# Half of the last product of a gated layer in seven quarter products instead of eight

## The chip, the cores and the metric

The kernel is written in Bass with Tile for one core of a Trainium2 chip: one launch, one core. The metric is the device time of a run in microseconds (us). Three runs of the kernel before were timed.

## What is computed

Three layers follow each other: a causal linear attention with decay, a soft mixture of experts, and a gated two-layer network. The change lies in the last one, whose input `x` (3072 tokens by 512) is the mixture's output `c @ slot_out` with 32 slots, so that the first product of the network has an inner rank of 32.

```
def _moe2_ref(x, w_in, w_out) -> np.ndarray:      # x 3072x512, w_in 512x2048, w_out 2048x512
    h = x @ w_in
    g = h * (1.0 / (1.0 + np.exp(-1.702 * h)))
    return (g @ w_out).astype(np.float32)
```

Both weights arrive as 64-bit floats.

## The kernel before

The first half of the program (attention and experts, up to about 162 us) is the same in both kernels. The rest is the last layer.

- **Splitting.** TensorE multiplies in fp32r, a rounded fp32. To keep precision, each factor is split into a rounded part (hi) and the remainder (lo), and three of the four products are formed: hi·hi, hi·lo, lo·hi.
- **Units.** The 3072 tokens are 6 blocks `b` of 512 (`NB`), the 2048 inner columns 16 tiles `f` of 128 (`KFF`). A unit `(b, f)` is one `h_unit` and one `o_unit`. `h_unit` forms h for 128 inner columns and 512 tokens with one matmul of 512 columns (`gst`, which holds `slot_out @ w_in` in hi and lo, against the softmax weights `cT`); ScalarE applies the gate twice, into `gh` (rounded) and `gg` (fp32). `lo_unit` has VectorE form `gl = gg - gh`. `o_unit` adds, for each of four tiles of 128 tokens, three matmuls of 512 columns to the sums `acc` in PSUM. That is 13 matmuls for each of 96 units.
- **Order.** `units` takes for each block first the tiles below `FA[b]` (2 for block 0, 4 for the others), whose sums are kept in `part`, then for each block the remaining tiles; `add_out` adds `part` to them and stores. h of unit u is issued two units ahead of its `o_unit`.
- **Narrowing.** `narrow` turns a piece of 64-bit weights into fp32 by three bit operations on VectorE (L151, L153, L155). For `w_out`, ScalarE then rounds it (L556) and GpSimd forms the remainder (L559). `work(budget)`, called between `h_unit` and `lo_unit` of each unit, takes such steps from a queue with costs until the budget `BUD` is used up. The raw weights come by DMA through three buffers. `make_g1` and `make_g2` make four tiles of `gst` at a time from narrowed `w_in`.
- **PSUM** has 8 banks: five in turn for `acc`, three for h and for small things.

Of the kernel before, what the change touches and what calls it, by code (L numbers as in the profile page):

```python
# [19 lines left out]
DM = H * D  # L20
# [16 lines left out]
FA = (2, 4, 4, 4, 4, 4)  # L37
# [5 lines left out]
BUD = 1.9  # L43
CW = (0.4, 0.6, 0.6, 0, 0.6)
# [4 lines left out]
def retention_soft_moe_mlp(  # L49
# [513 lines left out]

    def win_ops(j, z, k0=0, k1=KDM, f0=0, f1=256):
# [4 lines left out]

    units = [(b, f) for b in range(NB) for f in range(FA[b])] + [(b, f) for b in range(NB) for f in range(FA[b], KFF)]  # L570

    def h_unit(u):
        b, f = units[u]
        hp = pf.tile([P, 512], F32, tag="h", name=f"h{u}", bufs=3)
        mm(hp, lhsT=gst[:, f * P:(f + 1) * P], rhs=cT[:, 512 * b:512 * b + 512], start=True, stop=True)  # L575
        gh = fp.tile([P, 512], F32R, tag="gh2", name=f"gh{u}")
        nc.scalar.activation(out=gh, in_=hp, func=AF.Gelu_apprx_sigmoid)  # L577
        gg = fp.tile([P, 512], F32, tag="gg", name=f"gg{u}")
        nc.scalar.activation(out=gg, in_=hp, func=AF.Gelu_apprx_sigmoid)  # L579
        gl = fp.tile([P, 512], F32R, tag="gl2", name=f"gl{u}")  # L580
# [6 lines left out]
    def add_out(b, t, c, a, store=True):  # L587
        ob = part[b][:, t, c]
        nc.vector.tensor_tensor(out=ob, in0=a[:, c], in1=ob, op=ALU.add)  # L589
        if store:  # L590
            r0 = b * 512 + t * P
            nc.sync.dma_start(out=out[r0:r0 + P, c], in_=ob)

    def o_unit(u, t0=0, t1=4, terms=(0, 1, 2)):
        b, f = units[u]
        _, gh, gl = g_hl[u]
        whi, wlo = wh[f], wl[f]
        first, last = f in (0, FA[b]), f in (FA[b] - 1, KFF - 1)
# [13 lines left out]
        split = u == len(units) - 1  # L612
        if split:
            add_out(b, 3, slice(0, DM), acc[3], store=False)
        for t in range(t0, t1 - 1 if split else t1):
# [3 lines left out]
            if f == FA[b] - 1:  # L619
# [343 lines left out]
```

## Time and profile before

| | |
|---|---|
| three runs | 462.16, 463.09, 465.32 us; median 463.09 |
| profiled execution, span from first to last instruction | 462.1 us |
| last layer, from its first h matmul | 162.2 us to the end |
| TensorE busy | 448.5 us, 97% of the span |
| VectorE, ScalarE, GpSimd busy | 220.2, 169.9, 69.6 us |

The page gives no time of its own for the profiled execution beside the span; the fastest run shown is 0.06 us above that span, the median 1.0 us. A busy TensorE is not a TensorE at its peak, since matmuls are pipelined: the pace is read from the starts of neighbouring matmuls.

### The profile page before, as it was taken

To read this page: it belongs to the slowest core of one execution; us is meant where nothing else is said; L and a number is where in the kernel's file an instruction comes from. 1 tells how busy PE (TensorE), PEld (TensorE's weight loads), DVE (VectorE), ACT (ScalarE), POOL (GpSimd) and SP (SyncE) were. 2 spreads that over 40 slices of the span, in tenths; PEclk is the share of its full clock that TensorE was granted. 3 is DMA by queue.
4 is the path that set the end of the run, shared out by engine and by line. 5 is a ranking of instruction groups with operands and counts; after the bars stand their busy time and mean duration, and the time that the engine had idled before them with its cause. 6 is when DMAs were issued, how large, how long until landed. Compare 5 with 4: busy or idle time off the path is not lost.

```text
span 462.1 us, 8629 instructions
## 1 busy us (share of the span) xinstructions
PE 448.5 (97%) x3572; PEld 347.9 (75%) x3572; DVE 220.2 (48%) x412; ACT 169.9 (37%) x342; POOL 69.6 (15%) x69
## 2 busy tenths in 40 slices
PE   8899999999999989999999999999999999999996
PEld 5687877877334468788888888888888888888885
DVE  2355665755465479869396424224224224224223
ACT  2233232333121265665663533333333333333330
POOL 3253443533000112210222200000000000000000
PEclk9899999999999999999999999999999999999999
DMA  8999999999899654725231002002002002002002
GB/s 297 406 354 408 369 396 406 356 404 349 321 423 400 271 193 172 262 84 196 96 116 67 0 1 92 1 0 92 1 0 92 0 0 92 0 2 91 0 1 91
DMA packets 23527, 79.73 MB, mean 173 GB/s; under 512 B 2560, under 2 KB 4000, under 8 KB 19904
## 3 DMA queue, kind: packets, MB, share of 16 engines
q1 hardware_dynamic: 23088, 78.65, 45.3%
q8 instruction: 28, 0.46, 0.4%
q10 hardware_dynamic: 288, 0.36, 0.3%
q0 software_dynamic: 112, 0.16, 0.1%
q14 instruction: 11, 0.09, 0.1%
HBM read 72.88 MB, written 6.29 MB: 171 GB/s over the span
## 4 chain that ended last, share of the span: by engine, by line
PE 85%; DMA 10%; DVE 1%; SPq 1%; issue 1%; ACT 1%; POOL 1%; DVEq 0%; ACTq 0%; POOLq 0%
PE acc L606 56%; DMA qt<-qt_dram 8%; PE h L575 5%; PE sc L199 4%; PE eo L499 3%; PE hp L474 3%; PE y L248 3%; PE y L244 2%; PE xp L269 2%; DMA ktv_first<-ktv_dram 1%; PE st L256 1%; PE op L355 1%; PE tq L510 1%; PE lp L301 1%; PE gp L531 1%
## 5 line engine op out<-in xcount | busy, mean ns | idle before, releaser
L606 PE MATMUL acc<-wo_hl,gh 128*128 128x512 f32 x766 | 236.9, 391 | 0.7 <-ACT gh L577 0.7
L606 PEld LDWEIGHTS acc<-wo_hl,gh 128*128 128x128 f32 x766 | 142.8, 188 | 30.9 <-ACT gh L577 1.0
L606 PE MATMUL acc<-wo_hl,gl 128*128 128x512 f32 x383 | 148.8, 390 | 0.3 <-DVE gl L585 0.3
L585 DVE TENSOR_TENSOR gl<-gg,gh 128x512 fp32r<-128x512 f32 x96 | 66.6, 693 | 151.0 <-ACT gg L579 150.9
L577 ACT ACTIVATE gh<-h 128x512 fp32r<-128x512 f32 x96 | 57.5, 599 | 153.7 <-PE h L575 151.9
L606 PEld LDWEIGHTS acc<-wo_hl,gl 128*128 128x128 f32 x383 | 71.9, 188 | 15.8 <-DVE gl L585 0.7
L579 ACT ACTIVATE gg<-h 128x512 f32<-128x512 f32 x96 | 57.0, 594 | 0.0
L203 DVE TENSOR_TENSOR pt<-sc,ca_t 128x512 f32<-128x512 f32 x44 | 28.3, 686 | 22.3 <-PE sc L199 22.3
L575 PE MATMUL h<-cT,gst 128*128 128x512 f32 x96 | 37.4, 392 | 0.2 <-DVE gst L525 0.2
L559 POOL TENSOR_TENSOR wo_hl<-wf,wo_hl 128x512 fp32r<-128x512 f32 x16 | 21.2, 1345 | 100.5 <-ACT wo_hl L556 100.5
L199 PEld LDWEIGHTS sc<-qt,ktv 64*128 64x128 f32 x320 | 20.2, 192 | 10.8 <-issue 7.0
L199 PE MATMUL sc<-qt,ktv 64*128 64x128 f32 x320 | 23.9, 290 | 4.3 <-DMA qt<-qt_dram 3.8
L225 POOL TENSOR_TENSOR tb<-ca_t 128x512 f32<-128x512 f32 x19 | 19.9, 1048 | 45.4 <-DVE xT L260 45.4
L248 PE MATMUL y<-pt,vt 128*64 128x128 f32 x352 | 24.1, 279 | 0.0
L217 POOL TENSOR_TENSOR vt<-ktv,ca_t 128x512 f32<-128x512 f32 x20 | 20.8, 1042 | 13.3 <-DMA ktv<-ktv_dram 5.0
L258 ACT COPY s_sb<-st 128x256 f32<-128x256 f32 x20 | 7.4, 372 | 39.6 <-PE st L256 39.6
L248 PEld LDWEIGHTS y<-pt,vt 128*64 128x64 f32 x352 | 18.8, 136 | 3.8 <-issue 3.2
L575 PEld LDWEIGHTS h<-cT,gst 128*128 128x128 f32 x96 | 18.0, 188 | 4.7 <-DVE gst L525 1.0
L280 ACT COPY x<-xp 128x512 f32<-128x512 f32 x23 | 13.5, 587 | 11.6 <-PE xp L269 5.0
L260 DVE TENSOR_TENSOR xT<-y,tb 128x512 f32<-128x512 f32 x19 | 13.1, 691 | 9.3 <-PE y L248 9.1
L589 DVE TENSOR_TENSOR part<-acc,part 128x512 f32<-128x512 f32 x24 | 15.1, 684 | 3.6 <-PE acc L606 3.6
L269 PE MATMUL xp<-cb_t,xT 128*128 128x128 f32 x96 | 15.7, 286 | 0.0
(160 smaller groups left out, 366.7 us busy)
## 6 DMA issues: line engine op xcount, KB each, us to landing
w<-w_dram SPq DMA_DIRECT2D x36, 512.0 KB, 7.6
w<-w_dram SPq DMA_DIRECT2D x14, 1024.0 KB, 8.6
ktv<-ktv_dram SPq DMA_DIRECT2D x20, 512.0 KB, 8.4
wi<-w_in_dram SPq DMA_DIRECT2D x7, 1024.0 KB, 5.0
wo<-w_out_dram SPq DMA_DIRECT2D x7, 1024.0 KB, 4.8
out_dram<-part SPq DMA_DIRECT2D x23, 256.0 KB, 2.2
qt<-qt_dram SPq DMA_DIRECT2D x21, 256.0 KB, 6.4
kt<-kt_dram SPq DMA_DIRECT2D x12, 256.0 KB, 7.6
```

The source lines that it names most:

```text
L199: mm(sc[hh][:, a, :], lhsT=kT[hh * D:(hh + 1) * D, a, :], rhs=q_[hh * D:(hh + 1) * D, a, :], start=True, stop=True)
L203: nc.vector.tensor_tensor(out=pt[hh], in0=sc[hh], in1=mask[:, None, :].to_broadcast([P, NP, P]), op=ALU.mult)
L217: nc.gpsimd.tensor_tensor(out=vt, in0=v_, in1=vs[:, c, :, None].to_broadcast([P, H, D]), op=ALU.mult)
L225: nc.gpsimd.tensor_tensor(out=tb_t[i], in0=tab, in1=gsc[:, :, c, None].to_broadcast([P, NP, P]), op=ALU.mult)
L248: mm(out_(a, hh ^ (a & 1)), lhsT=vt[:, 2 * a + (hh ^ (a & 1)), :], rhs=pt[hh ^ (a & 1)][:, a, :], start=(c == 0 and a < 2), stop=True, ski ...
L269: nc.tensor.transpose(xp[:, a * P:(a + 1) * P], xT_t[i][:, a, :], ident)
L559: nc.gpsimd.tensor_tensor(out=l, in0=w, in1=h.bitcast(F32), op=ALU.subtract)
L575: mm(hp, lhsT=gst[:, f * P:(f + 1) * P], rhs=cT[:, 512 * b:512 * b + 512], start=True, stop=True)
L577: nc.scalar.activation(out=gh, in_=hp, func=AF.Gelu_apprx_sigmoid)
L579: nc.scalar.activation(out=gg, in_=hp, func=AF.Gelu_apprx_sigmoid)
L585: nc.vector.tensor_tensor(out=gl, in0=gg, in1=gh.bitcast(F32), op=ALU.subtract)
L606: mm(acc[t], lhsT=g[:, t * P:(t + 1) * P], rhs=w, start=first and n == 0, stop=n == 2 and (last or (u == len(units) - 2 and t == 3)))
```

## The change

The inner tiles 0 to 7 keep their plain units. For the tiles 8 to 15 (`SF0` on) the product `g @ w_out` is formed in Winograd's variant of Strassen's scheme: a square of two inner tiles by 256 tokens by 512 output columns is cut into 2x2 quarters, and seven products of sums of quarters take the place of eight.

- A new unit `("s", (e, j))` covers a block `e` of 256 tokens (12 of them) and a pair `j` of inner tiles (`NSP` = 4): 48 units. `s_h` makes two h matmuls of 256 columns, ScalarE applies the gate once into four quarters of `F_`, VectorE forms four sums of them; `s_round` (ScalarE) rounds seven quarters, `s_lo` forms their remainders: for the first four such units on VectorE alone, then two of seven on GpSimd and five on VectorE. `s_prod` issues 7 products of 3 matmuls with 256 columns each.
- The seven sums of a block stay in PSUM over the four pairs, in half banks (`HALF`): even blocks in banks 0 to 3, odd ones in 3 to 6; h has bank 7. `s_copy` and `s_combine` join them on ScalarE and VectorE into `X_` while the next block runs, and a GpSimd DMA with `accum_op` adds `X_` to the output in HBM, for ten of twelve blocks.
- The weights of the pairs need sums too: `w_sums` on GpSimd (four of 256 columns), then `w_hi` on ScalarE and `w_lo` on GpSimd for seven quarters.
- The order is now: 42 plain units (`runs`: the sums of each run go through `sg` to HBM by a DMA from ScalarE's queue, or by an accumulating one from GpSimd's), then the 48 new units, then the 6 plain units left of block 0, which end the program with `part`, `X_` and the accumulators.
- Narrowing is done in pieces of 1024 columns instead of two of 512; `BUD` falls from 1.9 to 1.2, and the steps that follow a piece on ScalarE and GpSimd are dealt out to later units (`at`, `due`). Each load is issued when a buffer is used up instead of all at once.

The diff, cut to its core:

```
-FA = (2, 4, 4, 4, 4, 4)
+NSP = 4
+SF0 = KFF - 2 * NSP
+LAG = 3
+PROD = ((0, 0, 0), (2, 0, 1), (6, 0, 2), (1, 1, 3), (4, 1, 0), (5, 1, 1), (3, 1, 2))
+HALF = (6, 3, 5, 4, 2, 0, 1)
+ORDER = (5, 6, 4, 1, 3, 2, 0)
...
-BUD = 1.9
-CW = (0.4, 0.6, 0.6, 0, 0.6)
+BUD = 1.2
...
+    def w_sums(j):
+        b = fr_t[SF0 // 2 + j]
+        t = ft_t[j] = fp.tile([P, 4, 256], F32, tag="ft", name=f"ft{j}", bufs=1)
+        tt = nc.gpsimd.tensor_tensor
+        tt(out=t[:, 0], in0=b[:, 0], in1=b[:, 1], op=ALU.subtract)
+        tt(out=t[:, 2], in0=b[:, 3], in1=b[:, 0], op=ALU.add)
+        tt(out=t[:, 1], in0=b[:, 3], in1=t[:, 0], op=ALU.add)
+        tt(out=t[:, 3], in0=b[:, 2], in1=t[:, 1], op=ALU.subtract)
...
+    def w_lo(j, z):
+        src, dst = (ft_t[j], WB[j]) if z else (fr_t[SF0 // 2 + j][:, 1:4], WA[j])
+        nc.gpsimd.tensor_tensor(out=dst[:, :, 1], in0=src, in1=dst[:, :, 0].bitcast(F32), op=ALU.subtract)
...
-    units = [(b, f) for b in range(NB) for f in range(FA[b])] + [(b, f) for b in range(NB) for f in range(FA[b], KFF)]
+    runs = [(0, 0, 2), (1, 0, 4), (2, 0, 4), (3, 0, SF0), (4, 0, SF0), (5, 0, SF0), (1, 4, SF0), (2, 4, SF0)]
+    punits = [(b, f) for b, f0, f1 in runs for f in range(f0, f1)]
...
+    seq = [("p", x) for x in punits] + [("s", x) for x in sunits] + [("q", (0, f)) for f in range(2, SF0)]
...
+    def s_h(u):
+        _, (e, j) = seq[u]
+        f, k = SF0 + 2 * j, u % LAG
+        hp = h_bank() if u < NP1 + 2 else flat(7)
+        for z in range(2):
+            mm(hp[:, 256 * z:256 * z + 256], lhsT=gst[:, (f + z) * P:(f + z + 1) * P],
+               rhs=cT[:, 256 * blocks[e]:256 * blocks[e] + 256], start=True, stop=True, skip_group_check=True)
+        F = F_[k]
+        nc.scalar.activation(out=F[:, 0:4].rearrange("p q t -> p (q t)"), in_=hp, func=AF.Gelu_apprx_sigmoid)
+        tt = nc.vector.tensor_tensor
+        tt(out=F[:, 4:6], in0=F[:, 0, None].to_broadcast([P, 2, P]), in1=F[:, 1:3], op=ALU.subtract)
+        tt(out=F[:, 6], in0=F[:, 1], in1=F[:, 5], op=ALU.subtract)
+        tt(out=F[:, 7], in0=F[:, 3], in1=F[:, 6], op=ALU.subtract)
+
+    def s_round(u):
+        k = u % LAG
+        nc.scalar.copy(out=GHL[k][:, 0], in_=F_[k][:, 1:8])
+
+    def s_lo(u):
+        k = u % LAG
+        n = 0 if u < NP1 + 4 else 2
+        for eng, c in ((nc.gpsimd, slice(0, n)), (nc.vector, slice(n, 7))):
+            if c.start == c.stop:
+                continue
+            eng.tensor_tensor(out=GHL[k][:, 1, c], in0=F_[k][:, 1:8][:, c], in1=GHL[k][:, 0, c].bitcast(F32),
+                              op=ALU.subtract)
...
+    def s_prod(u, i, n):
+        _, (e, j) = seq[u]
+        g, w, a = PROD[i]
+        ghl, wf = GHL[u % LAG], (WA[j], WB[j])[w][:, a]
+        p = slot_of(e, i)
+        mm(pv[:, p], lhsT=ghl[:, n // 2, g], rhs=wf[:, n % 2], start=j == 0 and n == 0 and (i in (5, 4, 3, 0)),
+           stop=j == NSP - 1 and n == 2, skip_group_check=True)
...
+    def s_combine(e, n):
+        y, x, h = Y_[0], X_[e % 2], 8 * (e % 2)
+        tt = nc.vector.tensor_tensor
+        if n == 0:
+            tt(out=y[:, 3], in0=pv[:, h], in1=y[:, 2], op=ALU.add)
+            tt(out=y[:, 0:2], in0=pv[:, h + 1:h + 3], in1=y[:, 3, None].to_broadcast([P, 2, 256]), op=ALU.add)
+        elif n == 1:
+            tt(out=x[:, 1:3], in0=pv[:, h + 2:h + 4], in1=y[:, 0:3:2], op=ALU.add)
+        else:
+            tt(out=x[:, 0:4:3], in0=pv[:, h + 4:h + 6], in1=y[:, 0:2], op=ALU.add)
+            b2 = blocks[e]
+            if b2 > 1:
+                nc.gpsimd.dma_start(out=out[256 * b2:256 * b2 + 256].rearrange("(t p) d -> p t d", p=P),
+                                    in_=x.rearrange("p (t c) d -> p t (c d)", c=2), accum_op=ALU.add)
...
+                for x, (i, n) in enumerate(order):
+                    s_prod(u, i, n)
+                    if x == 2 and j == NSP - 1:
+                        s_copy(e)
+                    if x == 8:
+                        if more:
+                            s_start(more)
+                        if s < NS1:
+                            s_round(s)
+                            s_lo(s)
+                if e > 0 and j < 3:
+                    s_combine(e - 1, j)
```

In the last loop u = s - 2: the products of unit s - 2 are issued in one step with the rounding and remainders of unit s and (`s_start(more)`) the h of unit s + 1.

TensorE late in the program, before: one unit and the start of the next (`acc_0` to `acc_3` are the four token tiles, `wo_hl` the split weights).

```order
L575 MATMUL h_3972<-cT,gst 128x512
L606 MATMUL acc_0_3876<-wo_hl_2134,gh_3934 128x512 x2
L606 MATMUL acc_0_3876<-wo_hl_2134,gl_3938 128x512
L606 MATMUL acc_1_3877<-wo_hl_2134,gh_3934 128x512 x2
L606 MATMUL acc_1_3877<-wo_hl_2134,gl_3938 128x512
...
L575 MATMUL h_3992<-cT,gst 128x512
```

TensorE after, two of the new units (`pb` is all of PSUM, `ghl` the split sums of g, `wa` and `wb` those of the weights).

```order
L760 MATMUL pb<-wb_2134,ghl_3366 128x256 x9
L729 MATMUL pb<-cT,gst 128x256 x2
L760 MATMUL pb<-wa_2133,ghl_3366 128x256 x3
L760 MATMUL pb<-wb_2134,ghl_3366 128x256 x3
L760 MATMUL pb<-wa_2133,ghl_3366 128x256 x6
L760 MATMUL pb<-wa_2135,ghl_3385 128x256 x3
L760 MATMUL pb<-wb_2136,ghl_3385 128x256 x6
L729 MATMUL pb<-cT,gst 128x256 x2
```

Thirteen matmuls of 512 columns have become 23 of 256, with the next h in the middle.

VectorE in the same stage, before: one subtraction for each unit, and sums only at the end of a block.

```order
L585 TENSOR_TENSOR gl_3342<-gg_3340,gh_3338 128x512
L589 TENSOR_TENSOR part_2126<-acc_0_3021,part_2126 128x512
L589 TENSOR_TENSOR part_2126<-acc_1_3022,part_2126 128x512
L589 TENSOR_TENSOR part_2126<-acc_2_3023,part_2126 128x512
L589 TENSOR_TENSOR part_2126<-acc_3_3024,part_2126 128x512
L585 TENSOR_TENSOR gl_3370<-gg_3368,gh_3366 128x512
```

VectorE after, two steps of the new stage (L734 to L736 are the sums of `s_h`, L748 the remainders, L775 and L777 parts of `s_combine`).

```order
L734 TENSOR_TENSOR F_3437<-F_3437 128x256
L735 TENSOR_TENSOR F_3437<-F_3437 128x128
L736 TENSOR_TENSOR F_3437<-F_3437 128x128
L748 TENSOR_TENSOR ghl_3385<-F_3365,ghl_3385 128x640
L775 TENSOR_TENSOR X_3441<-pb,Y 128x512
L734 TENSOR_TENSOR F_3365<-F_3365 128x256
L735 TENSOR_TENSOR F_3365<-F_3365 128x128
L736 TENSOR_TENSOR F_3365<-F_3365 128x128
L748 TENSOR_TENSOR ghl_3438<-F_3437,ghl_3438 128x640
L777 TENSOR_TENSOR X_3441<-pb,Y 128x2x256
```

One instruction in a unit has become four or five.

GpSimd while the weights are narrowed, before: two remainders for each pair of tiles of `w_out`.

```order
L559 TENSOR_TENSOR wo_hl_2135<-wf_2935,wo_hl_2135 128x512
L559 TENSOR_TENSOR wo_hl_2135<-wf_2936,wo_hl_2135 128x512
```

GpSimd after, one pair of the tiles 8 to 15 (`fr` is the narrowed pair, `ft` its sums).

```order
L594 TENSOR_TENSOR ft_2911<-fr_2820 128x256
L595 TENSOR_TENSOR ft_2911<-fr_2820 128x256
L596 TENSOR_TENSOR ft_2911<-fr_2820,ft_2911 128x256
L597 TENSOR_TENSOR ft_2911<-fr_2820,ft_2911 128x256
L605 TENSOR_TENSOR wa_2131<-fr_2820,wa_2131 128x3x256
L605 TENSOR_TENSOR wb_2132<-ft_2911,wb_2132 128x4x256
```

VectorE's row in that time, after: in four units a piece of `w_out` and one of `w_in`.

```order
L156 TENSOR_SCALAR fr_2713<-wo_2559 128x1024
L158 SCALAR_TENSOR_TENSOR fr_2713<-wo_2559,fr_2713 128x1024
L658 TENSOR_TENSOR gl_2710<-gg_2709,gh_2708 128x512
L160 SCALAR_TENSOR_TENSOR fr_2713<-wo_2559,fr_2713 128x1024
L658 TENSOR_TENSOR gl_2732<-gg_2731,gh_2730 128x512
L156 TENSOR_SCALAR win_2667<-wi_1_2646 128x1024
L158 SCALAR_TENSOR_TENSOR win_2667<-wi_1_2646,win_2667 128x1024
L658 TENSOR_TENSOR gl_2754<-gg_2753,gh_2752 128x512
L160 SCALAR_TENSOR_TENSOR win_2667<-wi_1_2646,win_2667 128x1024
L658 TENSOR_TENSOR gl_2781<-gg_2780,gh_2779 128x512
```

GpSimd's two instructions have become six with 2816 instead of 1024 columns, beside VectorE's larger pieces.

## Rows read from the trace of the kernel before

**Rows 1.** The page: busy time by engine, and the chain that ended last by line

```profile
PE 448.5 (97%) x3572; PEld 347.9 (75%) x3572; DVE 220.2 (48%) x412; ACT 169.9 (37%) x342; POOL 69.6 (15%) x69
...
PE acc L606 56%; DMA qt<-qt_dram 8%; PE h L575 5%; PE sc L199 4%; PE eo L499 3%; PE hp L474 3%; PE y L248 3%; PE y L244 2%; PE xp L269 2%; DMA ktv_first<-ktv_dram 1%; PE st L256 1%; PE op L355 1%; PE tq L510 1%; PE lp L301 1%; PE gp L531 1%
```

**Rows 2.** Waits of TensorE: us in total, times, longest

```profile
PE acc L606 <- ACT gh L577: 0.7, 1, 0.7
...
PE acc L606 <- DVE gl L585: 0.3, 1, 0.3
```

**Rows 3.** Timeline of one steady unit: start, duration (us), engine, line, instruction

```profile
302.19 0.39 PE L575 MATMUL h<-cT,gst 128*128 128x512 f32 x1
...
303.73 0.69 DVE L585 TENSOR_TENSOR gl<-gg,gh 128x512 fp32r<-128x512 f32 x1 [2.25 <-ACT gg L579]
...
305.13 0.39 PE L575 MATMUL h<-cT,gst 128*128 128x512 f32 x1
```

**Rows 4.** Timeline of the last six matmuls, of 256 columns: the first, the sixth

```profile
457.23 0.40 PE L627 MATMUL rest<-wo_hl,gh 128*128 128x256 f32 x2
...
457.82 0.28 PE L627 MATMUL rest<-wo_hl,gl 128*128 128x256 f32 x1
```

**Rows 5.** Timeline of TensorE at `make_g1` (L531) and `make_g2` (L543, L544; 128 columns)

```profile
192.81 1.08 PE L531 MATMUL gp<-win,A 128*32 128x128 f32 x32
...
196.90 0.22 PE L543 MATMUL rp<-Gh,selhl 128*128 128x128 f32 x1
196.96 0.28 PE L544 MATMUL rp<-Gl,selhl 128*128 128x128 f32 x1
...
197.63 0.28 PE L544 MATMUL rp<-Gl,selhl 128*128 128x128 f32 x1
197.74 0.69 PE L606 MATMUL acc<-wo_hl,gh 128*128 128x512 f32 x2
```

**Rows 6.** Groups by line and form, 188 us on: busy us, mean ns of one

```profile
L585 DVE TENSOR_TENSOR gl<-gg,gh 128x512 fp32r<-128x512 f32 x89 | 61.7, 694 | 148.7 <-ACT gg L579 148.6
...
L620 ACT COPY part<-acc 128x512 f32<-128x512 f32 x16 | 9.2, 593 | 1.4 <-PE acc L606 0.6
L153 DVE SCALAR_TENSOR_TENSOR wf<-wo,wf 128x512 uint32<-128x512 uint32 x12 | 7.8, 683 | 0.0
...
L151 DVE TENSOR_SCALAR wf<-wo 128x512 uint32<-128x512 uint32 x12 | 4.5, 418 | 0.0
...
L589 DVE TENSOR_TENSOR part<-rest,part 128x256 f32<-128x256 f32 x2 | 0.7, 416 | 0.0
```

**Rows 7.** VectorE subtractions of 128 columns (L400): min/median/max ns

```profile
L400 DVE TENSOR_TENSOR csb<-c,csb x6: 291/292/294, 139.2 to 141.6; 128x128 fp32r<-128x128 f32 x6
```

**Rows 8.** GpSimd's remainders (L559): min/median/max ns

```profile
L559 POOL TENSOR_TENSOR wo_hl<-wf,wo_hl x16: 1279/1292/1610, 158.0 to 264.3; 128x512 fp32r<-128x512 f32 x16
```

**Rows 9.** Timeline of VectorE: two that depend on each other, two that don't

```profile
149.82 0.69 DVE L153 SCALAR_TENSOR_TENSOR win<-wi,win 128x512 uint32<-128x512 uint32 x1
150.54 0.69 DVE L155 SCALAR_TENSOR_TENSOR win<-wi,win 128x512 uint32<-128x512 uint32 x1
...
181.33 0.68 DVE L153 SCALAR_TENSOR_TENSOR win<-wi,win 128x512 uint32<-128x512 uint32 x1
181.93 0.68 DVE L585 TENSOR_TENSOR gl<-gg,gh 128x512 fp32r<-128x512 f32 x1
```

**Rows 10.** Timeline of VectorE and GpSimd where their instructions overlap

```profile
192.31 0.68 DVE L585 TENSOR_TENSOR gl<-gg,gh 128x512 fp32r<-128x512 f32 x1
...
192.52 2.87 POOL L559 TENSOR_TENSOR wo_hl<-wf,wo_hl 128x512 fp32r<-128x512 f32 x2 [11.39 <-ACT wo_hl L556]
...
194.91 1.02 DVE L585 TENSOR_TENSOR gl<-gg,gh 128x512 fp32r<-128x512 f32 x1
```

**Rows 11.** DMA issues: KB each, median us to landing

```profile
wi<-w_in_dram SPq DMA_DIRECT2D x7, 1024.0 KB, 5.0
...
out_dram<-part SPq DMA_DIRECT2D x23, 256.0 KB, 2.2
```

More of the change, by code (lines that the diff above doesn't have):

```diff
@@ L601, in o_unit @@
             for t in range(t0, t1):
-                acc[t] = pf.tile([P, DM], F32, tag="acc", name=f"acc{u}_{t}", bufs=5)
+                acc[t] = acc_bank() if kind == "p" else flat(QBANK[t])
         def term(t, n):
             g, w = ops[n]
-            mm(acc[t], lhsT=g[:, t * P:(t + 1) * P], rhs=w, start=first and n == 0, stop=n == 2 and (last or (u == len(units) - 2 and t == 3)))
+            mm(acc[t], lhsT=g[:, t * P:(t + 1) * P], rhs=w, start=first and n == 0,
+               stop=n == 2 and (last or final or (u == NSEQ - 2 and t == 3)))
         if u == 0:
@@ L611, in o_unit @@
                     term(t, n)
[L612 to L615, printed above, removed]
+        if final:
+            add_out(3, slice(0, DM), acc[3], store=False)
+        for t in range(t0, t1 - 1 if final else t1):
             if u > 0:
@@ L618, in o_unit @@
                     term(t, n)
-            if f == FA[b] - 1:
-                nc.scalar.copy(out=part[b][:, t], in_=acc[t])
-            if f == KFF - 1:
-                add_out(b, t, slice(0, DM), acc[t])
-        if split:
-            for c in (slice(0, 256), slice(256, 512)):
-                rest = pf.tile([P, DM], F32, tag="acc", name=f"rest{c.start}", bufs=5)
+            if last and b == 0:
+                nc.scalar.copy(out=part[0][:, t], in_=acc[t])
+            elif last:
+                sg = fp.tile([P, DM], F32, tag="sg", name=f"sg{b}_{f}_{t}", bufs=4)
+                if t % 2 and u > 2 * len(punits) // 3:
+                    nc.vector.tensor_copy(sg, acc[t])
+                else:
+                    nc.scalar.copy(out=sg, in_=acc[t])
+                r0 = b * 512 + t * P
+                if f < 4 or b > 2:
+                    stores.append((out[r0:r0 + P], sg))
+                else:
+                    nc.gpsimd.dma_start(out=out[r0:r0 + P], in_=sg, accum_op=ALU.add)
@@ L840, in retention_soft_moe_mlp @@
+        todo.append(first_pair)
+        add_win(1, 0)
+        add_win(1, 1)
+        add_g(1)
+        add_pair(2)
+        add_pair(3)
+        for j in (2, 3):
+            add_win(j, 0)
+            add_pair(2 * j)
+            add_win(j, 1)
             add_g(j)
-            add_wout(4 * j + 2)
+            add_pair(2 * j + 1)
         todo.reverse()
-        queue = []
+        queue, now = [], [0]
         def work(budget):
             while budget > 0:
-                if not queue:
+                while not queue:
@@ L853, in work, with due @@
                 budget -= c
-        NU = len(units)
-        kw["out"] = pf.tile([P, 512], F32, tag="acc", name="kw2", bufs=5)
+        def due(u):
+            now[0] = u
+            for x in sorted(k for k in later if k <= u):
+                for fn in later.pop(x):
+                    fn()
+        kw["out"] = flat(4)
         h_unit(0)
```

273 lines of the change are left out of this document (208 added, 65 removed).

## The prediction

> **What bounds the kernel now.** I read the page first: TensorE is busy 97% of the span, and the chain that ended last runs 56% of the span through the matmuls of `o_unit` and 5% through those of h [rows 1]. A busy TensorE may still wait, so the waits of TensorE come next: in 96 units the last product waited 0.7 us for the gate and 0.3 us for the subtraction [rows 2], once each. The reader is to see that nothing but TensorE's own row of matmuls sets the end of this layer, and that VectorE with 48% busy has time in it. Then the timeline gives the price of a unit: h of one unit starts at 302.19, that of the next at 305.13 us [rows 3], so 13 matmuls of 512 columns take 2.94 us, 0.226 us each, though a single one is drawn 0.39 us long. What the change saves must come out of this row, and what it costs will show as TensorE waiting in it.
>
> **TensorE: 48 new units.** Two plain units for 512 tokens have 26 matmuls of 512 columns; for the same work the new kernel has two new units (256 tokens, two inner tiles) of 21 products and 2 for h, all of 256 columns. So one new unit stands against one plain unit. A matmul of 256 columns isn't half of one with 512 for certain, since each loads its own weights. The trace has six in a row, at the very end, with the same operands and a weight load each: the first starts at 457.23, the sixth at 457.82 us [rows 4], 0.118 us apart (0.116 to 0.120 by the rounding of the starts). The new unit is then 23 x 0.118 = 2.71 us, 0.23 less than 2.94, and 48 of them save 10.8 us (8.6 to 13.1). That the pace is near a floor is seen at 128 columns: from 196.96 to 197.63 us six steps take 0.112 us each [rows 5], so a half of the columns again saves next to nothing. I take 0.118, the row of the same shape. The six plain units at the end and the last tile are the same as before, and so is all up to 162 us.
> [...]
>
> **VectorE and GpSimd in the new units.** VectorE's subtraction takes 0.292 us for 128 columns [rows 7] and 0.694 for 512 [rows 6], so 1.05 ns a column more: 0.83 for 640 and 1.23 for 1024; 256 have a row, 0.416 [rows 6]. An instruction that needs the one before starts 0.03 us after its end, another 0.08 us before it (0.72 and 0.60 us apart at 0.69 and 0.68) [rows 9]. Per unit the three sums are 0.45 + 0.32 + 0.21 = 0.98 us and the remainders 0.75; the joins of a block add 0.45 + 3 x 0.61 = 2.3 us per four units. Four units: 4 x 1.73 + 2.3 = 9.2 us of VectorE against 4 x 2.71 = 10.9 us of TensorE. So VectorE goes from one instruction a unit to 85% and stays behind TensorE's row by itself. But GpSimd's share counts too. Where GpSimd starts a remainder at 192.52 while VectorE's subtraction runs, its two take 2.87 us instead of 2 x 1.28 [rows 8, 10], and VectorE's next one, begun at 194.91 beside the second, takes 1.02 instead of 0.69: 0.33 us lost by each, so the two exclude each other when both read from SBUF. GpSimd's two quarters (256 columns at 1.28 us for 512, so 0.64) cost 2.6 us per four units; all in series that is 11.8 us, 0.9 more than TensorE needs. The joins read PSUM and one operand of SBUF, and VectorE has 1.7 us free, together 4.0 us, into which 2.6 can fall. The cost lies between 0 and 11 groups of four units x 0.9 = 10 us; I take 0.5, near the fitting case, because the remainders of a unit are due 1 to 2 us before the products need them and VectorE may run late by that without harm.
> ScalarE has one gate (0.59), one rounding of 896 columns (at most 1.04 by proportion) and a quarter of a copy in 2.71 us (512 columns at 0.593, L620) [rows 6]: 1.8 us, hidden.
>
> **The plain units in which the weights are prepared.** Here the same exclusion has more to bite on. Four plain units hold one piece of `w_out` and one of `w_in`: the first step of a piece lies between 0.42 and 0.84 us (0.418 for 512 columns [rows 6]; I take 0.7), the other two 1.23 each by the slope above. Two pieces are 6.3 us, four subtractions 2.8, less 0.08 for each of ten: 8.3 us. GpSimd has 2816 columns for such a pair, at 2.5 ns 7.0 us. In series 15.3 us. TensorE needs 4 x 2.94 and, every other time, a `make_g1` and `make_g2` (1.08 us, and 0.84 from 196.90 to 197.74 [rows 5]): 12.7 us. So VectorE may fall behind by 2.6 us for each pair, three times over (the fourth pair's GpSimd work comes when narrowing is done): 7.8 us. It has a lead: the subtraction that starts at 303.73 ends 2.2 us after its h starts [rows 3], and its product is third in a row that starts two units and one h later, at 6.6 us: a lead of 4.3 us. Behind a late narrowing step on VectorE stands the `gl` of the next unit, and TensorE waits for that. 7.8 - 4.3 = 3.5 us of waiting. It is 0 if GpSimd is the one that falls behind, since nothing needs its results until the 43rd unit, and 6 if all four pairs count (10.4 - 4.3). I take 3.5, between them.
>
> **What else moves.** At the change from plain to new units the first products go into banks that the last plain run still holds: one copy on ScalarE (0.59 us) and one on VectorE stand before them; 0 to 1.3 us, I take 0.5. Stores from ScalarE's queue come four to a run; ScalarE has 2 x 0.59 us of gates in 2.94, so they are hidden, with the same lead as cover. The accumulating transfers (512 KB) have no row; a load of 1 MB lands in 5.0 us, a store of 256 KB in 2.2 [rows 11]. `X_` is written again seven units later, 19 us, so they cost nothing unless one takes four times the load of 1 MB. Loads are issued later than before, but each waited for its buffer anyway. The stream of tiles 4 to 7 of `gst` is due earlier (unit 14), where the order has made it one unit ahead.
>
> **Sum.** -10.8 + 0.5 + 3.5 + 0.5 = -6.3 us against the span of 462.1 us: 455.8. The median of the runs lies 1.0 us above that span, so 456.8 us.
>
> **Rivals.** *No price for the shared reads:* GpSimd falls behind instead of VectorE, and its quarters fit. Then -10.8 + 0.5 remains: 452.8 us, down to 450 at a pace of 0.116. For it speaks that nothing waits for GpSimd while the weights are prepared; against it that rows 10 show VectorE giving way.
> *VectorE and GpSimd become the bound, the other side:* each new unit's GpSimd quarters start just when VectorE could start its five, as both wait for the same rounding, so they run in series. Then 6 us in the plain units and 10 in the new ones: -10.8 + 6 + 10 + 0.5 = +5.7, 468.8 us. It decides from the point where four units of VectorE with what GpSimd takes from them pass 10.9 us, that is when more than 1.7 of the 2.6 us fall on remainders and sums. For it speaks that 9.2 is not far from 10.9; against it the joins' 2.3 us. [...]
> *The pace doesn't hold over thousands:* six matmuls are few. At 0.128 us a new unit is 2.94, and nothing is saved; with the 4.5 us of waits that is 467.6. Halfway, at 0.123 (2.83), 48 x 0.11 - 4.5 = 0.8 saved: 462.3 us, within 1%. The steady row of 512, 0.226 each for 96 units, and a floor of 0.112 below speak against it.
>
> **How the numbers follow.** A per cent, 4.6 us, is about what a measurement of this kernel can tell from no change. The forecast (453.5 to 458.4) gets 0.47, no price for the shared reads (449 to 453.5) 0.20, the cases that end within 1%, by a slower pace or by half of the shared price, 0.20, the slower case 0.13. So faster 0.67, same 0.20, slower 0.13; the likeliest alone is 453.5 to 458.4. The range from 450 to 463 leaves out the slower cases and a little below.
>
> **What would show it.** In the new units: h matmuls 2.71 us apart, waits of TensorE near 0, VectorE's share near 85 to 100%, remainders over 0.83 us where GpSimd's lie beside them. In the plain units 15 to 30: TensorE waiting for `gl`, some 3.5 us, after VectorE's first steps of a piece ran long beside GpSimd. Wrong would be: h more than 2.8 us apart without waits (the pace), waits of products for the remainders (VectorE as bound), or `X_` waiting for a transfer.

## The result, and the profile after

| | before | after |
|---|---|---|
| runs | 463.13 us median (461.7 to 469.31, 20 runs) | 468.67 us median (465.71 to 473.65, 20 runs) |
| ratio | | 1.0111 (95%: 1.0082 to 1.0139) |
| profiled execution, span | 462.1 us | 464.8 us (run 466.61) |

The change makes the kernel 1.1% slower, where 456.8 us, 1.4% faster, was forecast; the time lies above the range. The ratio and its interval are taken from the runs within 1.5% of the fastest of their kernel (19 before, 18 after), so the ratio is a little below the quotient of the medians, 1.0120.

How much of a span belongs to the change has to be read by stages, since the part ahead of the last layer, which the change doesn't touch, takes a different time in each execution: in the ten profiles of the kernel after and of the experiments the first h matmul starts anywhere from 161.1 to 170.1 us, with a lower granted clock where it is late (a mean of 0.986 in the execution that starts the layer at 170.1 us, 1.0 at 161.1), while the plain and the new units behind it repeat to 0.1 us where their code is the same. So here are both kernels cut at the same work: the 42 plain units, the 48 units whose form changes, the six units left and the end. First before (columns: length, busy time and count of each engine, granted clock, share of the DMA engines, GB/s).

```profile
162.20:299.50 137.30, 136.07 (x730) 111.06 (x731) 85.70 (x141) 72.56 (x139) 19.95 (x15) 1.00 0.31 108
299.50:440.90 141.40, 141.40 (x625) 117.09 (x624) 42.44 (x64) 52.18 (x96) 0.00 (x0) 1.00 0.08 30
440.90:462.10 21.20, 17.20 (x79) 14.18 (x77) 6.16 (x10) 4.35 (x8) 0.00 (x0) 1.00 0.14 50
```

The same view after:

```profile
core 0: us, PE busy (x) PEld busy (x) DVE busy (x) ACT busy (x) POOL busy (x), PEclk, DMA share, GB/s
161.10:300.90 139.80, 137.03 (x732) 110.89 (x733) 105.66 (x113) 77.21 (x139) 54.68 (x35) 1.00 0.44 143
300.90:442.70 141.80, 134.88 (x1103) 132.75 (x1102) 134.70 (x231) 73.93 (x106) 48.42 (x57) 1.00 0.30 46
442.70:464.80 22.10, 17.45 (x80) 14.35 (x78) 10.31 (x16) 5.43 (x10) 0.00 (x0) 1.00 0.14 49
```

The new units, for which 11 us less were forecast, take 141.8 us, 0.4 more than the plain units they replace. The plain units in which the weights are prepared take 2.5 more, the end 0.9 more, the part ahead happened to take 1.1 less: together the 2.7 us between the spans. In the middle stage VectorE is busy for 134.7 of 141.8 us, where it was busy for 42.4. The page says it as well: VectorE has 22% of the chain that ended last, where it had 1%; TensorE's share falls from 85% to 63%. The shares of the chain before:

```profile
PE 85%; DMA 10%; DVE 1%; SPq 1%; issue 1%; ACT 1%; POOL 1%; DVEq 0%; ACTq 0%; POOLq 0%
```

Busy time and chain after:

```profile
PE 443.4 (95%) x4052; PEld 363.2 (78%) x4052; DVE 336.4 (72%) x556; ACT 197.4 (42%) x354; POOL 152.7 (33%) x145
...
PE 63%; DVE 22%; issue 7%; DMA 6%; ACT 1%; POOL 0%; SPq 0%; DVEq 0%; ACTq 0%; POOLq 0%
```

The waits of TensorE [rows 2] name the two places: the remainders of the new units, ten times, and `gl` of the plain units.

```profile
PE pb L760 <- DVE ghl L748: 6.9, 10, 0.8
...
PE pb L687 <- DVE gl L658: 1.9, 4, 0.9
```

What happens ten times is seen in the timeline of one of them. Ahead of it an undisturbed unit shows the pace [rows 3, 4]: the h matmuls are 2.76 us apart, 23 matmuls at 0.120 us.

```profile
342.22 0.40 PE L729 MATMUL pb<-cT,gst 128*128 128x256 f32 x2
...
344.34 0.74 POOL L748 TENSOR_TENSOR ghl<-F,ghl 128x256 fp32r<-128x256 f32 x1 [2.10 <-issue]
344.43 0.93 DVE L734 TENSOR_TENSOR F<-F 128x256 f32<-128x256 f32 x1
...
344.98 0.40 PE L729 MATMUL pb<-cT,gst 128*128 128x256 f32 x2
...
346.10 0.94 ACT L740 CAST ghl<-F 128x896 fp32r<-128x896 f32 x1
...
347.65 1.20 POOL L780 DMA_DIRECT2D out_dram<-X  x1 [2.57 <-DVE X L777]
347.72 0.29 DVE L735 TENSOR_TENSOR F<-F 128x128 f32<-128x128 f32 x1
...
348.04 1.74 DVE L736 TENSOR_TENSOR F<-F 128x128 f32<-128x128 f32 x1
...
348.41 1.21 POOL L748 TENSOR_TENSOR ghl<-F,ghl 128x256 fp32r<-128x256 f32 x1
...
349.70 0.81 DVE L748 TENSOR_TENSOR ghl<-F,ghl 128x640 fp32r<-128x640 f32 x1
...
350.57 0.62 PE L760 MATMUL pb<-wb,ghl 128*128 128x256 f32 x3 [0.76 <-DVE ghl L748]
```

Two things are to be seen. At 344.34 GpSimd's two quarters run beside a sum of VectorE, which takes 0.93 us instead of 0.42: this is the price that the prediction knew. At 347.65 GpSimd issues the accumulating transfer, after a wait for VectorE's join; the 1.20 us of the issue are what is called the writing of a transfer below. The next two quarters stand behind it. They start at 348.41, 1.37 us after their rounding ended (346.10 + 0.94), and are drawn from there, while the transfer is still being written, with 1.21 instead of 0.74 us. VectorE's sum of 128 columns beside them takes 1.74 instead of 0.29 us, the remainders come late, and TensorE waits. The ends of the rows say more than their lengths: the quarters end 0.77 us after the issue (0.76 to 0.78 in the ten), which is about their own 0.74, and the sum ends 0.16 us after the quarters, as it does, at 0.15 us, in all 13 places of this stage where a quarter without a transfer ahead of it holds a sum of 128 columns. Read so, nothing is stretched on GpSimd; VectorE's sum is held until the quarters are through, and the issue puts that off. There are ten such transfers, and TensorE waits ten times; between the starts of matmuls nine gaps are 0.83 to 0.92 us longer than 0.120, one 0.38.

The spread of three groups (min/median/max ns) shows that most are undisturbed: the medians of VectorE are those of an instruction by itself [rows 6, 7], the maxima are not.

```profile
L734 DVE TENSOR_TENSOR F<-F x48: 410/422/942, 293.9 to 434.7; 128x256 f32<-128x256 f32 x48
L736 DVE TENSOR_TENSOR F<-F x48: 291/294/1743, 294.7 to 435.4; 128x128 f32<-128x128 f32 x48
L748 POOL TENSOR_TENSOR ghl<-F,ghl x44: 737/803/1217, 309.6 to 437.3; 128x256 fp32r<-128x256 f32 x44
```

The transfers themselves land in 5.6 us [rows 11], long before `X_` is written again, as the prediction has it.

```profile
out_dram<-X POOLq DMA_DIRECT2D x10, 512.0 KB, 5.6
```

### The profile page after: what moved, and what is told of

Its sections match the earlier page's. It is cut to its first block, busy times and chain, and to the rows that moved or that the text cites. A ratio compares the mean times of both kernels' runs of the same rounds, so it can differ in the third digit from the quotient of the medians.

```text
span 464.8 us, 9939 instructions
## 1 busy us (share of the span) xinstructions
PE 443.4 (95%) x4052; PEld 363.2 (78%) x4052; DVE 336.4 (72%) x556; ACT 197.4 (42%) x354; POOL 152.7 (33%) x145
## 4 chain that ended last, share of the span: by engine, by line
PE 63%; DVE 22%; issue 7%; DMA 6%; ACT 1%; POOL 0%; SPq 0%; DVEq 0%; ACTq 0%; POOLq 0%
PE pb L687 24%; PE pb L760 8%; DMA qt<-qt_dram 6%; DVE ghl L748 6%; PE sc L204 5%; DVE F L734 4%; PE y L253 4%; PE eo L504 3%; PE hp L479 3%; DVE F L735 2%; PE y L249 2%; PE pb L643 2%; PE xp L274 2%; DVE gl L658 2%; PE st L261 1%
## 5 line engine op out<-in xcount | busy, mean ns | idle before, releaser
L687 PE MATMUL pb<-wo_hl,gh 128*128 128x512 f32 x336 | 104.1, 392 | 0.7 <-ACT gh L652 0.7
L760 PE MATMUL pb<-wb,ghl 128*128 128x256 f32 x576 | 89.2, 285 | 6.9 <-DVE ghl L748 6.9
L760 PEld LDWEIGHTS pb<-wb,ghl 128*128 128x128 f32 x576 | 77.4, 191 | 9.0 <-DVE ghl L748 8.9
L687 PEld LDWEIGHTS pb<-wo_hl,gh 128*128 128x128 f32 x336 | 62.4, 188 | 13.5 <-ACT gh L652 1.0
L760 PE MATMUL pb<-wa,ghl 128*128 128x256 f32 x432 | 67.6, 283 | 0.0
L687 PE MATMUL pb<-wo_hl,gl 128*128 128x512 f32 x168 | 65.5, 393 | 1.9 <-DVE gl L658 1.9
L748 POOL TENSOR_TENSOR ghl<-F,ghl 128x256 fp32r<-128x256 f32 x44 | 38.4, 873 | 64.0 <-ACT ghl L740 42.1
L760 PEld LDWEIGHTS pb<-wa,ghl 128*128 128x128 f32 x432 | 58.9, 192 | 0.0
L740 ACT CAST ghl<-F 128x896 fp32r<-128x896 f32 x48 | 45.0, 938 | 11.9 <-DVE F L736 11.4
L748 DVE TENSOR_TENSOR ghl<-F,ghl 128x640 fp32r<-128x640 f32 (+1 forms) x48 | 41.9, 874 | 0.1
L736 DVE TENSOR_TENSOR F<-F 128x128 f32<-128x128 f32 x48 | 32.7, 681 | 1.6
L734 DVE TENSOR_TENSOR F<-F 128x256 f32<-128x256 f32 x48 | 28.8, 599 | 3.8 <-ACT F L732 3.8
```

The lines of the kernel that those rows point to most:

```text
L734: tt(out=F[:, 4:6], in0=F[:, 0, None].to_broadcast([P, 2, P]), in1=F[:, 1:3], op=ALU.subtract)
L736: tt(out=F[:, 7], in0=F[:, 3], in1=F[:, 6], op=ALU.subtract)
L740: nc.scalar.copy(out=GHL[k][:, 0], in_=F_[k][:, 1:8])
L748: eng.tensor_tensor(out=GHL[k][:, 1, c], in0=F_[k][:, 1:8][:, c], in1=GHL[k][:, 0, c].bitcast(F32), op=ALU.subtract)
L760: mm(pv[:, p], lhsT=ghl[:, n // 2, g], rhs=wf[:, n % 2], start=j == 0 and n == 0 and (i in (5, 4, 3, 0)), stop=j == NSP - 1 and n == 2, sk ...
```

## The experiments

All are edits of the changed kernel; times of a stage are read as in the windows above. The first four ran together, beside 13 runs of the kernel before (median 463.71 us).

**All remainders on VectorE.**

```
-        n = 0 if u < NP1 + 4 else 2
+        n = 0
```

> All seven remainders of every new unit on VectorE, none on GpSimd; the accumulating transfers stay. In the changed kernel's trace the 48 new units take 141.8 us: 1104 matmuls at 0.120 are 132.5, the rest is ten waits of about 1 us. Theory A (GpSimd's quarters hold VectorE up: L734 takes 0.94 instead of 0.42 where a quarter runs beside it): VectorE's four units are 4 x (0.42 + 0.29 + 0.29 + 1.10) + 2.5 of joins = 10.9 us against TensorE's 11.04, nearly all waits go, the stage takes 133 to 136 us, the run 459 to 463 us beside the changed kernel's 464.8 + 1.8. Theory B (VectorE's own work is too much, whoever runs beside it): 256 columns more for each unit are 4 x 0.27 us, the stage takes 150 us or more, the run 475 or more. Theory C (the ten accumulating transfers, whose issue takes GpSimd 1.2 us, stop VectorE): ten waits of about 1 us stay, the stage keeps 140 to 143 us.

Measured: 459.93 us median (456.91 to 466.57, 4 runs), ratio 0.9878 (0.9795 to 0.9961). The profiled execution reached the last layer late (170.1 us). The window of its new units:

```profile
309.90:442.30 132.40, 132.40 (x1103) 132.29 (x1102) 117.77 (x231) 71.17 (x106) 14.27 (x13) 1.00 0.31 49
```

The new units take 132.4 us, 1104 times 0.120, and TensorE never waits in them. VectorE has more columns and is busy for 17 us less. Theory B, that VectorE's own work is too much, is out. The ten transfers are issued here too, and VectorE's sums stay at their least time beside them:

```profile
L736 DVE TENSOR_TENSOR F<-F x48: 291/291/293, 303.7 to 434.4; 128x128 f32<-128x128 f32 x48
...
L780 POOL DMA_DIRECT2D out_dram<-X x10: 1188/1197/1201, 331.8 to 431.2; - x10
```

So a transfer alone doesn't hold VectorE, against theory C as far as it stands alone: 0.293 us is the longest of these 48 sums.

**GpSimd's quarters left out.**

```
-            if c.start == c.stop:
+            if c.start == c.stop or (eng is nc.gpsimd):
```

> GpSimd's two remainders of the new units are left out from the fifth unit on (the products use those of earlier units, so the low parts of two of seven sums are wrong); VectorE's five and the transfers stay as they are. Theory A: this takes away all that GpSimd's quarters cost; VectorE's four units fall to 4 x (0.42 + 0.29 + 0.29 + 0.82) + 2.5 = 9.8 us, the waits go but for one or two, stage 133 to 135 us, run 458 to 460. Theory B: VectorE has the same instructions, 140 to 142 us in the stage, run 466. Theory C: waits of 0.5 to 1 us beside each of the ten transfers stay unless VectorE's new slack covers them: 133 to 139.

Measured: 457.73 us median (457.13 to 459.52, 4 runs), ratio 0.9861 (0.9800 to 0.9922); 132.3 us in the new units, no wait. It says the same as the run before it: without the quarters the transfers cost nothing. And with 107.0 us of VectorE instead of 117.8 the stage is no shorter, so 132.3 is TensorE's own row.

**Plain stores in place of the transfers.**

```
-                nc.gpsimd.dma_start(..., in_=x..., accum_op=ALU.add)
+                nc.sync.dma_start(..., in_=x...)
```

> The ten joined blocks are stored from SyncE's queue without being added to what lies in the output (the sums of the plain units are overwritten there), so GpSimd issues no transfer in the stage; its quarters stay. Theory A: at most a part of the waits go, as the quarters stay: 138 to 142 us in the stage, run 464 to 467. Theory C: the ten waits go, 132.5 to 134 us in the stage, run 457 to 459. Theory B: no change, 141 to 142.

Measured: 459.03 us median (455.77 to 462.4, 10 runs), ratio 0.9891 (0.9856 to 0.9927); 132.3 us in the new units, no wait. All quarters are still on GpSimd and still hold VectorE up, by 0.44 us in most units:

```profile
L735 DVE TENSOR_TENSOR F<-F x48: 291/731/787, 299.7 to 430.5; 128x128 f32<-128x128 f32 x48
...
L748 POOL TENSOR_TENSOR ghl<-F,ghl x44: 736/741/808, 314.9 to 432.3; 128x256 fp32r<-128x256 f32 x44
```

That price fits into VectorE's room and TensorE never sees it. So theories A and C, each by itself, both fail: the quarters without the transfers are free, the transfers without the quarters are free, and together they cost 9 us. What remains is that they meet (theory D below).

**Joins beside the quarters.**

```
                             s_round(s)
+                            if e > 0 and j < 3:
+                                s_combine(e - 1, j)
                             s_lo(s)
-                if e > 0 and j < 3:
-                    s_combine(e - 1, j)
+                        elif e > 0 and j < 3:
+                            s_combine(e - 1, j)
```

> The join of three units in four is issued on VectorE between the sums of the next unit and the remainders, so that it may run beside GpSimd's quarters (a join reads one operand from PSUM). Theory A: three quarters of GpSimd's time (3 x 0.74 of 3.3 us in four units) falls on joins, VectorE's four units fall from 11.8 to about 10.5 us, stage 133 to 136, run 459 to 462. Theory B: the order in VectorE's row gives nothing, 141 to 143, and the remainders come 0.7 us later, so up to 146 us in the stage. Theory C: no change, 141 to 143.

Measured: 471.9 us median (468.23 to 475.7, 4 runs), ratio 1.0131 (1.0060 to 1.0202); 145.2 us in the new units, 3.4 more than in the changed kernel. Theory A's expectation is missed by 9 us or more. The timeline shows why: the join of the third unit, and with it the transfer, now stands ahead of that unit's own remainders, so two pairs of quarters run behind the transfer (L748 x2) and one sum of 256 columns on VectorE takes 2.61 us instead of 0.42. TensorE waits 19 times in place of ten, 7.8 us in all.

```profile
349.28 1.20 POOL L780 DMA_DIRECT2D out_dram<-X  x1 [4.15 <-DVE X L777]
349.63 2.61 DVE L734 TENSOR_TENSOR F<-F 128x256 f32<-128x256 f32 x1
350.05 1.91 POOL L748 TENSOR_TENSOR ghl<-F,ghl 128x256 fp32r<-128x256 f32 x2
```

This edit moved two things at once, the join and the transfer, which makes it a weak test of what it was meant for; for the meeting of transfer and quarter it is a dose: more quarters behind the transfer, a longer hold.

**The transfer one place later.** This run, the slower narrowing and the version with both edits ran beside 17 runs of the kernel before (median 463.15 us). `held` is a list that the transfer is put into and issued from behind the next unit's `s_lo`.

```
-                nc.gpsimd.dma_start(out=..., in_=x..., accum_op=ALU.add)
+                held.append(lambda: nc.gpsimd.dma_start(out=..., in_=x..., accum_op=ALU.add))
...
                             s_lo(s)
+                        while held:
+                            held.pop()()
```

> GpSimd keeps its two quarters of each new unit and the ten accumulating transfers, but issues each transfer behind the next unit's quarter instead of ahead of it. In the changed kernel the transfer waits for the join on VectorE and the quarter stands behind it: the quarter begins 1.3 us after its rounding is done, takes 1.21 instead of 0.74, and VectorE's sum beside it takes 1.74 instead of 0.29. Theory D (this collision is what costs; neither quarters nor transfers do by themselves): the ten waits of 0.92 us go, the stage takes 132.3 to 134 us instead of 141.8, the run about 457 to 459. Theory E (the two loads add up wherever the transfer stands, as VectorE has only 0.5 us free in four units): waits of 0.5 to 1 us stay in most blocks, stage 137 to 142, run 462 to 467.

Measured: 458.43 us median (456.9 to 460.58, 4 runs), ratio 0.9876 (0.9823 to 0.9929). The same instructions, with ten of them one place further on in GpSimd's row:

```profile
346.67 0.74 POOL L748 TENSOR_TENSOR ghl<-F,ghl 128x256 fp32r<-128x256 f32 x1 [2.04 <-issue]
...
346.81 0.74 DVE L735 TENSOR_TENSOR F<-F 128x128 f32<-128x128 f32 x1
...
347.35 1.20 POOL L780 DMA_DIRECT2D out_dram<-X  x1
...
347.59 0.29 DVE L736 TENSOR_TENSOR F<-F 128x128 f32<-128x128 f32 x1
...
349.43 0.77 POOL L748 TENSOR_TENSOR ghl<-F,ghl 128x256 fp32r<-128x256 f32 x1 [0.88 <-ACT ghl L740]
```

The transfer is written while no quarter is due, VectorE's sum beside it takes 0.29 us, and the stage is 132.4 us:

```profile
302.00:434.40 132.40, 132.40 (x1103) 132.30 (x1102) 124.81 (x231) 71.17 (x106) 46.72 (x57) 1.00 0.31 49
```

Theory D holds, theory E is out: 9.4 us of the stage hang on the place of ten instructions in one queue. The moving of the data isn't what holds VectorE either: these transfers land 5.4 us after their issue (median), so the quarter at 349.43 runs while the data move, and it takes 0.77 us, within the 0.74 to 0.81 of the run with plain stores.

**A late quarter without a transfer.** In the changed kernel the quarter behind the transfer is also late, as the transfer waits for the join. Does lateness do it, or the overlap? On top of the plain stores:

```
+                nc.gpsimd.tensor_tensor(out=Y_[1], in0=x[:, 0, 0:1], in1=x[:, 0, 1:2], op=ALU.subtract)
                 nc.sync.dma_start(..., in_=x...)
```

> As the run with plain stores from SyncE's queue (the additions into the output are left out again), but where the changed kernel has a transfer on GpSimd there stands a subtraction of one column that waits for the same join, so that the quarter behind it is late as in the changed kernel, with no transfer being written. Theory G (the hold comes from a quarter that runs while GpSimd writes a transfer): the quarters are 0.74 to 0.81 us long, VectorE's sums at most 0.95, no waits of TensorE, 132.3 to 133 us in the stage. Theory H (lateness is enough: a quarter that starts 0.5 to 1.3 us late meets VectorE where it has no room): a VectorE sum of 1.3 us or more and a wait of 0.5 to 0.9 us in each block stay, 138 to 142 us.

One run, 461.05 us, beside one of the kernel before at 465.16; 132.3 us in the new units, no wait. The quarter stands behind a join as it did, and VectorE's sum beside it takes 0.85 us, not 1.74. The second view has the longest such sum of the run, 0.872 us.

```profile
348.53 0.94 ACT L740 CAST ghl<-F 128x896 fp32r<-128x896 f32 x1
...
348.79 0.69 DVE L777 TENSOR_TENSOR X<-pb,Y 128x512 f32<-128x512 f32 x1
...
349.55 0.31 POOL L780 TENSOR_TENSOR scr<-X 128x1 f32<-128x1 f32 x1 [1.89 <-DVE X L777]
349.81 0.73 POOL L748 TENSOR_TENSOR ghl<-F,ghl 128x256 fp32r<-128x256 f32 x1
349.84 0.85 DVE L735 TENSOR_TENSOR F<-F 128x128 f32<-128x128 f32 x1
```

```profile
L736 DVE TENSOR_TENSOR F<-F x48: 291/293/872, 298.8 to 429.7; 128x128 f32<-128x128 f32 x48
```

That is what theory G expected, but for quarters of up to 0.89 us. It is not the lateness of the changed kernel, though: the quarter starts 0.34 us after its rounding ends (0.25 to 0.49 in the ten), not 1.37. Theory H was tried at less than the delay it names, so this run alone doesn't rule it out. What speaks for theory G beyond it are the lengths: without a transfer ahead, a quarter adds at most 0.58 us (0.872 - 0.291) to a VectorE instruction, whichever of a unit's three sums and its remainders it meets in this run and the others, while behind a transfer it adds 1.45 us, each of ten times, to a sum that starts 0.37 us before the quarter and by its own 0.29 would be over by then. Being late decides which instruction a quarter meets, but nothing of that length was seen without a transfer. The difference, 0.9 to 1.0 us, is of the size of the wait that TensorE has once for each transfer.

**Slower narrowing.** In the changed kernel the plain units wait where GpSimd's long instructions meet VectorE's narrowing:

```profile
239.31 2.84 POOL L605 TENSOR_TENSOR wb<-ft,wb 128x1024 fp32r<-128x1024 f32 x1
...
239.82 2.88 DVE L156 TENSOR_SCALAR fr<-wo 128x1024 uint32<-128x1024 uint32 x1
...
242.74 1.23 DVE L158 SCALAR_TENSOR_TENSOR fr<-wo,fr 128x1024 uint32<-128x1024 uint32 x1
...
243.88 0.68 DVE L658 TENSOR_TENSOR gl<-gg,gh 128x512 fp32r<-128x512 f32 x1
...
244.62 0.50 PE L687 MATMUL pb<-wo_hl,gl 128*128 128x512 f32 x1 [0.89 <-DVE gl L658]
```

A step that takes 0.68 us where GpSimd rests takes 2.88, and the `gl` behind it is late for its product. The last of these GpSimd instructions ends at 268.5 us and the new units begin at 300.9, so the steps can be spread:

```
-                work(BUD)
+                work(BUD if s < 14 else 0.7)
```

> From the 14th unit on one narrowing step in a unit (a budget of 0.7) instead of two and one in turn, so that the weights are ready near the 38th plain unit instead of the 31st; the new units are as in the changed kernel. Theory F (VectorE falls behind in the plain units because GpSimd's long instructions hold its narrowing steps up: 2.88 instead of 0.68 us beside a remainder of 1024 columns): with three units for a piece in place of two VectorE catches up between them, the three waits of TensorE for gl (0.35 to 1.05 us, 2 us in all) go, the plain units take 137.5 to 138 us instead of 139.8, the run is 2 us below the changed kernel's 466.6. Rival: the waits come from the lengths of single steps (a step of 2.9 us ahead of a gl), whatever lies between, and stay: 139.5 to 140 us, or more if the last pieces are late for the new units.

Measured: 466.61 us median (464.81 to 469.2, 10 runs), ratio 1.0059 (1.0024 to 1.0095); the plain units take 138.4 us, 1.4 less. The three waits between 243 and 259 us are gone, as theory F has it, but a new one of 0.9 us stands at 294 us (what it is, the next run shows), which leaves the stage above F's 137.5 to 138. The new units stay at 141.9 us.

**Both.** All remainders on VectorE, and the slower narrowing.

> All seven remainders on VectorE, and one narrowing step in a unit from the 14th on. If the two prices are apart from each other, the plain units take 137.5 to 138 and the new ones 132.3 us, together 11.5 us less than in the changed kernel: a run of 454.5 to 457, 1.5% below the kernel before. If VectorE's stretched narrowing runs into the new units, whose remainders are now all on it, 1 to 3 us of that are lost: 456 to 460.

Measured: 456.35 us median (456.06 to 458.55, 6 runs), ratio 0.9837 (0.9791 to 0.9883). The gains add up: 138.4 us in the plain units, 132.3 in the new ones. But the wait at the end of the plain units is there as well, and its timeline shows the meeting again, in another stage: four transfers of plain sums are written, and the last two remainders of the weights, behind them in GpSimd's row, start before that is over.

```profile
287.08 3.60 POOL L712 DMA_DIRECT2D out_dram<-sg  x4 [4.03 <-ACT sg L707]
...
289.60 2.94 POOL L605 TENSOR_TENSOR wa<-fr,wa 128x768 fp32r<-128x768 f32 x1
...
289.80 6.25 DVE L658 TENSOR_TENSOR gl<-gg,gh 128x512 fp32r<-128x512 f32 x2 [1.18 <-ACT gg L653]
```

The last row joins two `gl`. The group's spread shows that one of them has nearly all of it, 5.65 us; the other takes its usual 0.68.

```profile
L658 DVE TENSOR_TENSOR gl<-gg,gh x42: 678/692/5649, 164.1 to 295.4; 128x512 fp32r<-128x512 f32 x42
```

**The remainders ahead of the transfers.** On top of both edits, beside 11 runs of the kernel before (median 462.91 us):

```
-                work(BUD if s < 14 else 0.7)
+                work(BUD if s < 20 else 0.7)
```

> As the version with both edits, but the narrowing runs at its old pace up to the 20th unit and at one step in a unit only from there, so that GpSimd's last two remainders are issued ahead of its four transfers near 286 us and not behind them. In the version with both edits those two remainders start while the transfers are being written (issue from 287.08 us for 3.60, remainders from 289.60), two gl on VectorE beside them take 6.25 us together instead of 1.4, and TensorE waits 0.9 us for one. Theory D in another stage (a GpSimd instruction that starts while a transfer is written holds VectorE for long): that wait goes, the plain units take 137.4 to 137.6 us instead of 138.4, the run about 1 us less, 455 to 456.5. If the hold comes from the length of the two remainders alone, or if the faster start brings back a wait near 245 us, the plain units take 138 to 139 us and the run stays at 456 to 457.

Measured: 455.53 us median (454.02 to 457.51, 6 runs), ratio 0.9839 (0.9803 to 0.9876). The last remainder now starts at 278.36 us, ahead of the transfers, and a `gl` that runs while the transfers are written takes its 0.69 us:

```profile
285.84 3.60 POOL L712 DMA_DIRECT2D out_dram<-sg  x4 [5.08 <-ACT sg L707]
...
288.04 0.69 DVE L658 TENSOR_TENSOR gl<-gg,gh 128x512 fp32r<-128x512 f32 x1 [0.65 <-ACT gg L653]
```

The wait is gone, and none came back near 245 us. The two remainders take 1.84 and 2.40 us here, the `gl` beside them 1.45 and 2.01 us, and TensorE waits for neither, so the length of the remainders alone is not the cause. The windows:

```profile
161.20:298.60 137.40, 136.20 (x733) 111.21 (x733) 100.16 (x113) 76.65 (x139) 50.62 (x35) 1.00 0.45 146
298.60:430.90 132.30, 132.30 (x1102) 132.20 (x1101) 117.67 (x231) 71.20 (x106) 14.21 (x13) 1.00 0.31 49
```

So theory D told what another stage would do. The plain units now take what they take in the kernel before, though all the weights are prepared in them, and the new units what their matmuls take. With 1.6% off the kernel before, this version and the one ahead of it are the best measured here; the profiles tell them apart by 1.0 us in that stage, the ratios don't.

## Why the prediction was wrong

- **What bounds the kernel, and the arithmetic of the change:** right. Before, TensorE's row alone set the end; with nothing in its way the new stage is 23 matmuls for each of 48 units.
- **The pace:** right in kind, sized a little too well. 945 of 1097 gaps between the stage's matmuls are 0.120 us, the upper end of what six rounded starts allowed. The saving is 141.4 - 132.4 = 9.0 us instead of 10.8. The rival of a pace that doesn't hold is out.
- **VectorE and GpSimd in the new units, 0.5 us of 0 to 10:** right in that the price of the quarters beside VectorE is small; the runs make it 0: a quarter stretches VectorE by 0.45 us or so, which its room takes up (plain stores, transfer later). The joins, which read one operand from PSUM, pay nothing, as was taken in counting their 2.3 us as room: 18 of them overlap a quarter in the changed kernel and take 0.68 or 0.69 us, as they do alone, and the quarters beside them their own 0.74. GpSimd's 256 columns were put at 0.64 us by proportion and take 0.74, which would have changed little.
- **The step that failed** is the accumulating transfers: "`X_` is written again seven units later, 19 us, so they cost nothing unless one takes four times the load of 1 MB". I costed them by where their data land and left out their issue, 1.20 us on GpSimd, with a wait for VectorE's join ahead of it and the next quarters behind it. That meeting cost 9.4 us (141.8 against 132.4), all that the new units save. It is the only step whose correction turns the sign: with the transfer one place later the same program runs in 458.4 us, inside the range.
- **The slower rival** gave 468.8 us, and the time came out there, but not by its mechanism: that the two agree is luck. Its sign, products that wait for the remainders, did come, ten times. It had VectorE's row too full, with quarters and remainders in series; VectorE is busy for 95% of the stage, and this look of a full engine would have confirmed it, had the run with plain stores, with the same quarters, not shown TensorE without a wait.
- **The plain units, 3.5 us of 0 to 6:** right in kind, a little large. TensorE waits for `gl` for 1.9 us, of which a first 0.3 [rows 2] was there before, and the stage is 2.5 us longer. The piling up behind a stretched step is what the timeline shows. What I took as given, that the steps must fall so close, was a choice of the order: spread further, they cost nothing.
- **The transition, 0.5 us:** TensorE waits for no copy there.
- **The end**, called the same, takes 22.1 us instead of 21.2; in the other profiles it takes 21.5 to 22.3. Half of the 0.9 us lies behind the issue of the last store, which ends 3.1 us ahead of the end of the span in the kernel after and 2.6 us in the one before; the rest is open.

Made again with what was measured, the sum is -9.0 + 9.4 + 2.5 + 0.9 = +3.8 us for the layer. The fastest runs of the two kernels differ by 4.0 us; the medians by 5.5, and what the 1.5 us between are is left open. The part ahead of the layer, which has nothing of the change in it, spreads by more than that.

What stays open as well is why VectorE's sum, which starts ahead of the quarter, is held already while the transfer is written, when the writing by itself holds nothing. The runs show that it takes both, and when the sum is let go, not by which path. Nor was a quarter as late as in the changed kernel tried without a transfer.

## What to carry to other kernels

A transfer that GpSimd issued stood in its row as an instruction of 1.20 us: cost a transfer's issue, what it waits for, and what stands behind it, before asking when its data land. A stage in which an engine looks 95% full may hang on ten instructions in the wrong place, so move one before taking work away. And where two engines meet, a price can be free while it fits into the room of the slower one, as the 0.44 us in most units of the run with plain stores did, until something else uses up that room.

## What was not expected of the hardware

- A GpSimd subtraction in line behind the issue of a transfer held a VectorE instruction with two inputs in SBUF through the rest of both: a sum of 128 columns took 1.74 us instead of 0.29 (the changed kernel), a sum of 256 columns with two pairs of quarters behind the transfer 2.61 instead of 0.42 (joins beside the quarters), a subtraction of 512 columns with two longer ones behind it 5.65 instead of 0.69 (both edits). The writing alone (1.20 us, or 3.60 for four) held none of them: with all remainders on VectorE the longest sums of 128 and 256 columns were 0.294 and 0.427 us, and in the last run a subtraction of 512 columns beside the four took 0.69.
- With a transfer or without, the held instruction ended about the same time after the subtraction that held it: 0.14 to 0.16 us for a sum of 128 columns, 0.28 or 0.29 for 256, 0.55 or 0.56 for a `gl` of 512.
- A narrowing step (one input, 1024 columns) beside a GpSimd subtraction took 2.88 us instead of 0.68 in the changed kernel: an instruction with one input was held too.
- fp32r matmuls of 256 columns started 0.120 us apart in 945 of 1097 gaps of the changed kernel's new units; those of 512 columns started 0.2267 us apart on average in the same stage before.
